# The last two batches of attention set between the steps of the leading expert's first product, and quarter-array products for all queries

## The chip, the core and the metric

The kernel runs on one core of one Trainium2 chip. The metric is the device time of that core in microseconds (us), from repeated executions. The engines are TensorE (PE, with its weight loads PEld), VectorE (DVE), ScalarE (ACT), GpSimd (POOL) and SyncE (SP), which here only issues transfers (DMA). Each engine works through its own instructions in order and waits on semaphores for the others.

## What is computed

Attention without a softmax, a normalisation per head, and then a mixture of eight experts of which each token takes one:

```python
def _attn_ref(q, k, v, g_norm):                 # q, k, v: 8 batches, 8 heads, 576 tokens, 64
    kv = np.einsum('bhsd,bhse->bhde', k, v)
    out = np.einsum('bhsd,bhde->bhse', q, kv)
    rms = np.sqrt(np.mean(out * out, axis=-1, keepdims=True) + 1e-06)
    return out / rms * g_norm

def _moe_ref(x, w_gate, w_output_gate, w1, w2): # x: 4608 tokens x 512; w1: 8 x 512 x 1024; w2: 8 x 1024 x 512
    logits = x @ w_gate
    e_idx = np.argmax(logits, axis=1)
    # gate_w: softmax probability of the chosen expert; eom: a sigmoid of x @ w_output_gate
    for e in range(E):
        mask = e_idx == e
        h = np.maximum(x[mask] @ w1[e], 0.0)
        out[mask] = gate_w[mask, None] * eom[mask, e, None] * (h @ w2[e])
```

## The kernel before

**Attention.** `p1_main` goes through the batches 0 to 7. `kv_part(b)` multiplies k and v of a batch (tile `kvps`, L474), ACT and DVE copy the result out (`aug`, `kvc`), `kvT_part` transposes it (`kvTps`), and `m_part` multiplies it with the two gates (`mps`, L501). The 4608 tokens are 36 tiles of 128 rows. `out_tile(g)` multiplies the queries of a tile with the `aug` of its batch (tile `ops`, L541), and ACT takes three pieces out of PSUM: the row itself (`xrow`, L546), its squares (`sq`, L548) and the gate products (`gp`, L549). DVE sums the squares (`ss`, L562). `ops`, `mps` and the experts' `hps` share two PSUM buffers of one pool, `ps_b`.

**Loads and stores.** All loads stand on SP's queue: k and v (`kvm`, four pieces of 512 KB to a batch, and `rem` for what remains), queries (`qT`, two tiles to a piece), and the weights (`wraw`). Rows `xrow` and their tails `xtail` are written to a table `xs` in HBM, from which an expert later gathers its rows (`xg`, an indirect DMA issued by POOL, L239). SP waits in order: a store that waits for its data holds all that is behind it.

**Routing.** The tiles form four groups of 10, 10, 4 and 12. `route(gi)` is a chain of small DVE operations for a group, with products on PE between (`rps`: counts; `tblps`: the table of rows, L749) and the operands `la` made by POOL, ACT and DVE (L719). It is a generator; `advance()` takes all open chains one stretch further, and the code calls it after each tile and at steps written out by hand. After the third group, that is after 24 tiles, the most loaded expert so far is known: the leading expert. Its first 384 rows are gathered (`gather(0)`), scaled by POOL (`xg`, L247), transposed (`tps`, L271) and split in a high and a low part (`xT`).

**Experts.** `RUNS` lists the stretches of rows: run 0 is the first 384 rows of the leading expert, run 1 its remaining 320, run 2 and on the other experts. `mm1(i, f)` is one of eight steps of the first product (`hps`, L308, twelve matmuls to a step); ACT and DVE make the high and low part of its result (`hT`, L317 and L318). `mm2(i, k)` is the second product for one tile of rows (`yps`, L350). Weights come as `wraw` and are split in `whi` (ACT, or DVE for the first) and `wlo` (DVE or POOL, L217 and L224); for the second product of the leading expert POOL makes all four `wlo`.

**What sets the order.** Inside `manual_schedule` the instructions of the named engines stay in the order in which the code issues them. Up to tile 36 the steps of the leading expert hang on the number of finished tiles (`HOOKS`: R is `advance`, G the gather, W the loads of w2, X the stores of the last rows, N the scaling, L one step of the leading expert, S one split of w2), and then the string `TAIL` sets them. `mm2(0, ...)` is issued after that, in the loop over `RUNS`, with the staging (`stage`) of run 1 between its matmuls; on PE its first ten matmuls come to stand ahead of the last three steps of the first product.

Of the kernel before, what the change touches and what calls it, by code (L numbers as in the profile page):

```python
# [11 lines left out]
F32 = mybir.dt.float32  # L12
# [9 lines left out]
P = 128  # L22
# [44 lines left out]

HOOKS = {15: 'R', 27: 'RR', 28: 'R', 31: 'RGW', 32: 'X', 34: 'NL'}
TAIL = "QLLLLRRRSLSRRSLLRRRLSLRRSRLSLL"
# [58 lines left out]
MAN = {ET.PE, ET.Activation, ET.DVE, ET.Pool}  # L131
# [3 lines left out]
def body(ctx: ExitStack, tc: tile.TileContext, kvm, rem, qT, wg, gn, w1, w2, kc, xs, tab, out):  # L135
# [191 lines left out]
    def mm2(i, k, events):  # L327
# [5 lines left out]
        ps = ps_y.tile([P, DM], F32, name="yps", tag=f"y{ny % 2}")  # L333
        ny += 1
# [18 lines left out]
        y = hp.tile([P, DM], F32, name="y", bufs=3)  # L353
# [11 lines left out]
        tc.add_to_no_dep_group("out", i_.ins)  # L365

# [80 lines left out]

    def load(spare):

        while loads and len(free) > spare:  # L450
            where, k, src = loads.pop(0)
            n = src.shape[0]
            if k in where:
                nc.sync.dma_start(out=where[k][P - n:], in_=src)
                continue
            t = take([P] + list(src.shape[1:]), F32, "ld")
            nc.sync.dma_start(out=t[:n], in_=src)
            where[k] = t
# [56 lines left out]
    def out_tile(g):  # L515
# [19 lines left out]
        for p in range(NP):  # L535
            for b, r0, m in parts:
                q0 = g % 2 * P + r0

                for u in range(2):
                    r = slice(u * D, (u + 1) * D)  # L540
                    nc.tensor.matmul(ps[r0:r0 + m, u, p * W:(p + 1) * W], qt[g // 2][r, p, q0:q0 + m],  # L541
                                     augs[b % 3][r, p, :], start=True, stop=True)
# [254 lines left out]
    def run_out(limit):  # L797
        nonlocal done_tiles
        if done_tiles < limit:
# [4 lines left out]
            advance()  # L804
# [3 lines left out]
            if lead_placed and opened[0] and (0, 1, 0) not in raw and (1, 0) not in wgt:  # L808
                for c in range(1):
                    wload(0, 1, c)  # L810
            for step in HOOKS.get(done_tiles, ""):
                act(step)

    def act(step):
        if step == "R":
            advance()
        elif step == "W":
            for c in range(4):
                wload(0, 2, c)
        elif step == "X":  # L820
            open_rows(1)
# [3 lines left out]
        elif step == "G":  # L825
            gather(0)
            behind.append(nc.gpsimd.memset(mark, 0.0))
            for c in range(1, 4):
                after_rows(wload(0, 1, c))
        elif step == "N":  # L830
            scale_rows(0)
        elif step == "S":
            next(lead2, None)
        else:
            next(lead, None)
# [337 lines left out]
```

## Time and profile before

| | us |
|---|---|
| median of three runs | 619.95 (618.67 to 620.07) |
| the profiled execution | 620.81 |
| its span, first to last instruction | 618.8 |
| PE busy | 566.5 (92%) |
| DVE, ACT, POOL busy | 263.2, 222.0, 164.0 |
| HBM read and written | 72.63 MB and 19.99 MB |

All durations come from the profiled execution, whose time lies 2.0 us above its span and 0.86 us above the median. A row of the timeline gives start, duration, engine, line, operation, tiles and sizes; in brackets stands the idle time of the engine before it and what ended it. The fp32 matmuls of the attention appear as two passes, so the counts there are double those of the program. PEclk is the clock that TensorE was granted, 1.00 being full speed.

### The profile page before, as it was taken

What the parts mean: (1) busy time and instruction counts of PE and PEld (TensorE: products, weight loads), DVE (VectorE), ACT (ScalarE), POOL (GpSimd) and SP (SyncE); (2) the same over time, 40 slices, a digit from 0 to 9 for tenths busy, and PEclk for the clock granted to TensorE, in tenths of its full rate; (3) what the DMA queues carried; (4) which work ended last, traced back from release to release, by engine and by line L of the source; (5) the groups of instructions that cost most, each with busy time, mean ns of one, the idle gap of its engine ahead of it and who ended that gap; (6) DMA issues with size and microseconds to landing.
All of it is one profiled execution on the core that took longest, in us unless ns stands there. A gap on an engine that the chain in (4) does not pass through costs nothing.

```text
span 618.8 us, 10459 instructions
## 1 busy us (share of the span) xinstructions
PE 566.5 (92%) x4179; PEld 506.3 (82%) x4179; DVE 263.2 (43%) x536; ACT 222.0 (36%) x413; POOL 164.0 (27%) x163
## 2 busy tenths in 40 slices
PE   3799978848999999999899999999999999999991
PEld 3688868747898998889789988998799889889881
DVE  2123688699425456225331453235135325424300
ACT  1335545634225334323331343234234423523310
POOL 2001044443832510630036117104500630110010
PEclk9958777579999999999999999999999999999996
DMA  8999991770564622349776332524432451110010
GB/s 271 367 409 407 405 366 49 246 285 7 166 231 138 202 89 90 87 169 35 16 159 199 115 122 91 172 69 138 145 112 74 135 181 68 53 52 2 0 47 14
DMA packets 39122, 92.53 MB, mean 150 GB/s; under 512 B 14418, under 2 KB 14546, under 8 KB 39072
## 3 DMA queue, kind: packets, MB, share of 16 engines
q1 hardware_dynamic: 32176, 71.63, 37.4%
q0 software_dynamic: 6464, 20.00, 10.2%
q8 instruction: 34, 0.56, 0.4%
q10 hardware_dynamic: 432, 0.21, 0.1%
q14 instruction: 16, 0.13, 0.1%
HBM read 72.63 MB, written 19.99 MB: 150 GB/s over the span
## 4 chain that ended last, share of the span: by engine, by line
PE 57%; issue 19%; DMA 10%; DVE 4%; POOL 3%; ACT 3%; another core or an unknown queue 2%; SPq 0%; POOLq 0%; DVEq 0%
PE hps L308 24%; PE yps L350 23%; PE ops L541 3%; PE kvps L474 3%; DMA ld<-kvm 3%; DMA xs<-xrow 2%; PE tps L271 2%; POOL out L361 2%; DMA ld<-qT 2%; DMA ld<-rem 2%; PE yps L345 1%; POOL xg L239 1%; DMA wraw<-w 1%; DMA xg<-xs,gidx 1%
## 5 line engine op out<-in xcount | busy, mean ns | idle before, releaser
L308 PE MATMUL hps<-xT,whi 128*128 128x320 f32 (+4 forms) x1024 | 197.3, 310 | 9.5 <-DVE hT L318 8.4
L350 PE MATMUL yps<-whi,hT 128*128 128x512 f32 (+2 forms) x592 | 195.9, 399 | 1.0 <-ACT whi L221 1.0
L308 PEld LDWEIGHTS hps<-xT,whi 128*128 128x128 f32 x1024 | 163.6, 191 | 11.9 <-DVE hT L318 9.1
L350 PEld LDWEIGHTS yps<-whi,hT 128*128 128x128 f32 (+2 forms) x592 | 111.3, 188 | 25.2 <-ACT whi L221 1.2
L308 PE MATMUL hps<-xT,wlo 128*128 128x320 f32 (+4 forms) x512 | 121.6, 309 | 0.0
L318 DVE SCALAR_TENSOR_TENSOR hT<-hps,hT 128x512 fp32r<-128x512 f32 (+5 forms) x112 | 59.2, 529 | 142.6 <-ACT hT L317 142.3
L350 PE MATMUL yps<-wlo,hT 128*128 128x512 f32 (+2 forms) x296 | 116.6, 394 | 0.8 <-DVE wlo L224 0.8
L317 ACT ACTIVATE hT<-hps 128x512 fp32r<-128x512 f32 (+5 forms) x112 | 52.5, 469 | 164.0 <-PE hps L308 121.6
L308 PEld LDWEIGHTS hps<-xT,wlo 128*128 128x128 f32 x512 | 89.0, 191 | 0.0
L361 POOL DMA_INDIRECT out<-y,oidx x42 | 44.8, 1068 | 154.2 <-ACT y L360 107.2
L239 POOL DMA_INDIRECT xg<-xs,gidx x42 | 43.2, 1029 | 137.5 <-PE tps L271 54.6
L350 PEld LDWEIGHTS yps<-wlo,hT 128*128 128x128 f32 (+2 forms) x296 | 55.7, 188 | 12.1 <-DVE wlo L224 1.1
L217 DVE SCALAR_TENSOR_TENSOR wlo<-wraw,gcol,whi 128x1024 fp32r<-128x1024 f32 x32 | 43.9, 1372 | 39.6 <-ACT whi L214 39.6
L247 POOL TENSOR_TENSOR xg<-xg 128x512 f32<-128x512 f32 (+3 forms) x40 | 44.0, 1102 | 43.9 <-DMA xg<-xs,gidx 43.5
L541 PE MATMUL ops<-aug,ld 64*128 64x80 f32 (+1 forms) x640 | 49.0, 327 | 5.8 <-ACT gp L549 5.7
L541 PEld LDWEIGHTS ops<-aug,ld 64*128 64x128 f32 (+1 forms) x640 | 44.5, 230 | 8.8 <-ACT gp L549 6.4
L360 ACT ACTIVATE y<-yps,tl 128x512 f32<-128x512 f32 (+2 forms) x37 | 25.5, 689 | 71.4 <-PE yps L350 68.4
L276 ACT CAST xT<-tps 128x512 fp32r<-128x512 f32 (+3 forms) x45 | 23.6, 530 | 67.6 <-PE tps L271 63.9
L277 DVE TENSOR_TENSOR xT<-tps,xT 128x512 fp32r<-128x512 f32 (+3 forms) x45 | 27.7, 617 | 46.9 <-ACT xT L276 43.3
L474 PE MATMUL kvps<-ld 128*64 128x64 f32 (+1 forms) x640 | 36.4, 300 | 11.1 <-DMA ld<-kvm 10.7
L474 PEld LDWEIGHTS kvps<-ld 128*64 128x64 f32 (+1 forms) x640 | 33.1, 209 | 14.0 <-DMA ld<-kvm 12.0
L224 DVE TENSOR_TENSOR wlo<-wraw,whi 128x1024 fp32r<-128x1024 f32 x28 | 34.3, 1226 | 13.5 <-ACT whi L221 6.7
(158 smaller groups left out, 403.2 us busy)
## 6 DMA issues: line engine op xcount, KB each, us to landing
wraw<-w SPq DMA_DIRECT2D x64, 512.0 KB, 3.2
ld<-kvm SPq DMA_DIRECT2D x32, 512.0 KB, 10.2
ld<-qT SPq DMA_DIRECT2D x18, 512.0 KB, 10.2
xs<-xrow SPq DMA_DIRECT2D x13, 512.0 KB, 10.4
xs<-xrow SPq DMA_DIRECT2D x2, 1280.0 KB, 15.2
ld<-rem SPq DMA_DIRECT2D x3, 512.0 KB, 10.2
xg<-xs,gidx POOLq DMA_INDIRECT x42
out<-y,oidx POOLq DMA_INDIRECT x42
```

What stands on the lines that cost most here:

```text
L217: eng.scalar_tensor_tensor(out=lo, in0=r, scalar=gcol[:, 0:1], in1=hi.bitcast(F32), op0=ALU.mult, op1=ALU.subtract)
L224: eng.tensor_tensor(out=lo, in0=r, in1=hi.bitcast(F32), op=ALU.subtract)
L239: nc.gpsimd.indirect_dma_start(out=x[:M, :], out_offset=None, in_=rows, in_offset=bass.IndirectOffsetOnAxis(ap=gidx[:M, p, t:t + 1], axis=0))
L247: eng.tensor_tensor(out=v, in0=v, in1=f, op=ALU.mult)
L277: nc.vector.tensor_tensor(out=lo[:, :, c0:c0 + M], in0=v, in1=hi.bitcast(F32)[:, :, c0:c0 + M], op=ALU.subtract)
L308: nc.tensor.matmul(ps[:, j, :n], w[:, o:o + P], x[d][:, j * N:j * N + n], start=(d == 0 and k == 0), stop=(d == 3 and k == 2))
L317: nc.scalar.activation(hh, x, AF.Relu)
L318: nc.vector.scalar_tensor_tensor(out=v(h[:, l:l + n]), in0=x, scalar=0.0, in1=hh.bitcast(F32), op0=ALU.max, op1=ALU.subtract)
L350: nc.tensor.matmul(ps[:M], a, b, start=(f == 0 and k == 0), stop=(f == 7 and k == 2))
L361: i_ = nc.gpsimd.indirect_dma_start(out=out, out_offset=bass.IndirectOffsetOnAxis(ap=oidx[:M, p, t:t + 1], axis=0), in_=y[:M], in_offset=N ...
L474: nc.tensor.matmul(ps[u * D:(u + 1) * D, p * D:(p + 1) * D], k, v, start=(s == 0 and p == 0), stop=(s == 4 and p == NP - 1))
L541: nc.tensor.matmul(ps[r0:r0 + m, u, p * W:(p + 1) * W], qt[g // 2][r, p, q0:q0 + m], augs[b % 3][r, p, :], start=True, stop=True)
```

## The change

The first 24 tiles and the batches 0 to 5 go as before, with no step of the leading expert among them. The loads of the last two batches and of the queries from tile 24 on go into a second list, `later`. Then a string, `SCRIPT`, sets everything until the end of the leading expert's first 384 rows: routing of the first three groups to its end (`QF`), five of the late loads, weights and the gather, batch 6 (`K`, `T`, `M`), and the eight steps of the first product with twelve tiles (`o`) and batch 7 among them. The splits of w2 and the routing of the last group come after the last tile, with the three `mm2(0, ...)` between the routing's stretches (`Y`). Run 1 is gathered, scaled and staged after that, by itself. SP joins the engines whose order is the code's. The products of `out_tile` are cut into quarters of the array: 64 query rows by 64 contraction rows each, instead of 128 by 64, which before was so only where a batch ended inside a tile. The second products of run 0 take their PSUM from `ps_b`.

```diff
-HOOKS = {15: 'R', 27: 'RR', 28: 'R', 31: 'RGW', 32: 'X', 34: 'NL'}
-TAIL = "QLLLLRRRSLSRRSLLRRRLSLRRSRLSLL"
+FIRST = LEAD_TILES
+SCRIPT = ("QF" "ddddd1G1" "K" "NL" "T" "LLL" "dd1" "L" "L" "MX" "o" "dd1" "L" "o" "dd" "L" "o" "o" "dd" "L" "o" "K"
+          "L" "T" "o" "dd" "L" "M" "o" "22" "o" "L" "o" "o" "22" "L" "o" "o" "S" "Q" "SRSRS" "YRRRR" "YRRRR" "YRRRRRR")
...
-MAN = {ET.PE, ET.Activation, ET.DVE, ET.Pool}
+MAN = {ET.PE, ET.Activation, ET.DVE, ET.Pool, ET.SP}
...
-        ps = ps_y.tile([P, DM], F32, name="yps", tag=f"y{ny % 2}")
-        ny += 1
+        if i == 0:
+            ps = ps_b.tile([P, 2, 512], F32, name="yps0", tag="big")[:, 0]
+        else:
+            ps = ps_y.tile([P, DM], F32, name="yps", tag=f"y{ny % 2}")
+            ny += 1
...
+    cut = lambda w, k: (k if w is qt else 2 * k if w is rt else k[0])
+    later = [l for l in loads if cut(l[0], l[1]) >= (FIRST // 2 if l[0] is qt else FIRST * P // S + 1)]
+    loads = [l for l in loads if not any(l is x for x in later)]
...
-                q0 = g % 2 * P + r0
-                for u in range(2):
-                    r = slice(u * D, (u + 1) * D)
-                    nc.tensor.matmul(ps[r0:r0 + m, u, p * W:(p + 1) * W], qt[g // 2][r, p, q0:q0 + m],
-                                     augs[b % 3][r, p, :], start=True, stop=True)
+                for c0 in range(r0, r0 + m, D):
+                    q0 = g % 2 * P + c0
+                    for u in range(2):
+                        r = slice(u * D, (u + 1) * D)
+                        nc.tensor.matmul(ps[c0:c0 + D, u, p * W:(p + 1) * W], qt[g // 2][r, p, q0:q0 + D],
+                                         augs[b % 3][r, p, :], start=True, stop=True)
...
-            advance()
+            if done_tiles <= FIRST:
+                advance()
...
+        elif step == "F":
+            while routing:
+                advance()
...
+        elif step in "12":
+            c = (w1s if step == "1" else w2s).pop(0)
+            d = wload(0, int(step), c)
+            if behind:
+                after_rows(d)
+        elif step == "d":
+            fetch(later)
+        elif step == "K":
+            state["kvc"] = kv_part(b)
...
+        elif step == "o":
+            run_out(NT)
...
+        elif step == "Y":
+            mm2(0, state.setdefault("y", 0), {})
...
-        for b in range(B):
-            lim = tiles_ready(b - 1) if b else 0
+        for b in range(B - 2):
+            lim = min(tiles_ready(b - 1) if b else 0, FIRST)
...
-        while done_tiles < NT:
-            run_out(NT)
-        for step in TAIL:
+        while done_tiles < FIRST:
+            run_out(FIRST)
+        for step in SCRIPT:
             act(step)
...
                 gather(1)
                 scale_rows(1)
-                for _ in lead:
-                    next(lead2, None)
-                for _ in lead2:
-                    pass
+                for h in hT[0]:
+                    give(h)
+                for x in range(len(tiles_of(1))):
+                    stage(1, x)
+                continue
```

Three places in the order of the instructions carry the prediction. The first is SP's queue around the third group's tails (`xtail` of 4 tiles, written when that group is routed). Before:

```order
L771 DMA xs<-xrow 128x2x512 x2
L771 DMA xs<-xtail 128x10x16
L771 DMA xs<-xtail 128x4x16
L185 TENSOR_LOAD epos
L185 ISA x2
L194 ISA
L194 DMA wraw<-w 128x1024
```

and after the change:

```order
L788 DMA xs<-xrow 128x2x512
L788 DMA xs<-xtail 128x10x16
L788 DMA xs<-xtail 128x4x16
L473 DMA ld<-rem 128x1024
L473 DMA ld<-kvm 128x1024 x4
L188 TENSOR_LOAD epos
L188 ISA x2
L197 ISA
L197 DMA wraw<-w 128x1024
```

The loads of batch 6 now stand behind the store that waits for the routing of group three, and ahead of the first weights of the leading expert.

The second is PE from the leading expert's transposes (`tps`) into its first product (`hps`). Before, the attention (`ops`) was done by then:

```order
L541 MATMUL ops<-aug_115,ld 64x80 x2
L541 MATMUL ops<-aug_116,ld 64x80 x2
L541 MATMUL ops<-aug_116,ld 128x80 x32
L271 MATMUL tps<-ident,xg 128x128 x12
L308 MATMUL hps<-xT,whi 128x384 x2
L308 MATMUL hps<-xT,wlo 128x384
```

After, of the eight steps of `hps` the first two are shown, the repeated rows left out:

```order
L490 MATMUL kvps<-ld 64x64 x40
L505 MATMUL kvTps<-ident,kvc 128x128 x2
L274 MATMUL tps<-ident,xg 128x128 x12
L311 MATMUL hps<-xT,whi 128x384 x2
L311 MATMUL hps<-xT,wlo 128x384
...
L517 MATMUL mps<-gw,kvT 64x16 x8
L558 MATMUL ops<-aug_117,ld 64x80 x16
L311 MATMUL hps<-xT,whi 128x384 x2
L311 MATMUL hps<-xT,wlo 128x384
...
L558 MATMUL ops<-aug_117,ld 64x80 x16
```

Batch 6's product now stands ahead of the transposes, and the tiles from 24 on stand between the steps.

The third is PE from the last `tblps` of the last group's routing to run 1's first product (`hps` of 320 columns). Before:

```order
L749 LDWEIGHTS la
L749 MATMUL tblps<-rrc,la 128x96
L308 MATMUL hps<-xT,whi 128x384 x2
...
L271 MATMUL tps<-ident,xg 128x128 x4
L350 MATMUL yps<-whi,hT 128x512
...
L271 MATMUL tps<-ident,xg 128x64 x4
L350 MATMUL yps<-whi,hT 128x512
...
L308 MATMUL hps<-xT,whi 128x320 x2
```

After:

```order
L356 MATMUL yps_2135<-whi,hT 128x512
L693 LDWEIGHTS row_106
...
L766 LDWEIGHTS la
L766 MATMUL tblps<-rrc,la 128x96
L356 MATMUL yps_2246<-whi,hT 128x512
...
L274 MATMUL tps<-ident,xg 128x128 x8
L274 MATMUL tps<-ident,xg 128x64 x4
L311 MATMUL hps<-xT,whi 128x320 x2
```

The table of the last group stood ahead of three steps of the first product and nearly all second products; now two of the three second products (`yps`) stand ahead of the counts (`row`, for `rps`), one behind the table, and the transposes of run 1 follow with nothing between them and its first product.

More of the change, by code (lines that the diff above doesn't have):

```diff
@@ L352, in mm2 @@
                 e()
-        y = hp.tile([P, DM], F32, name="y", bufs=3)
+        y = take([P, DM], F32, "y0") if i == 0 else hp.tile([P, DM], F32, name="y", bufs=3)
         if M == T:
@@ L365, in mm2 @@
         tc.add_to_no_dep_group("out", i_.ins)
+        if i == 0:
+            give(y)
     def lead_run():
@@ L446, in body, with fetch @@
                 nq += 1
+    cut = lambda w, k: (k if w is qt else 2 * k if w is rt else k[0])
+    later = [l for l in loads if cut(l[0], l[1]) >= (FIRST // 2 if l[0] is qt else FIRST * P // S + 1)]
+    loads = [l for l in loads if not any(l is x for x in later)]
+    later.sort(key=lambda l: (12.5 + (l[1] - FIRST // 2) // 2 if l[0] is qt else 2 * l[1] + 0.1 if l[0] is rt else 2 * l[1][0]))
     def load(spare):
         while loads and len(free) > spare:
[L451 to L458, printed above, removed]
+            fetch(loads)
+    def fetch(loads):
+        where, k, src = loads.pop(0)
+        n = src.shape[0]
+        if k in where:
+            nc.sync.dma_start(out=where[k][P - n:], in_=src)
+            return
+        t = take([P] + list(src.shape[1:]), F32, "ld")
+        nc.sync.dma_start(out=t[:n], in_=src)
+        where[k] = t
     def kv_part(b):
@@ L807, in run_out @@
                 open_rows(0)
[L808 to L812, printed above, removed]
+    w1s, w2s = list(range(4)), list(range(4))
+    state = {"b": B - 2}
     def act(step):
+        b = state["b"]
         if step == "R":
             advance()
[L817 to L821, printed above, removed]
+        elif step == "F":
+            while routing:
+                advance()
         elif step == "Q":
@@ L849, in p1_main @@
                 run_out(lim)
-        while done_tiles < NT:
-            run_out(NT)
-        for step in TAIL:
+        while done_tiles < FIRST:
+            run_out(FIRST)
+        for step in SCRIPT:
             act(step)
+        assert not later and done_tiles == NT and not w1s and not w2s and state["y"] == len(tiles_of(0))
         while routing:
             advance()
+        for _ in lead:
+            assert False
+        for _ in lead2:
+            assert False
     vec = nc.vector
@@ L1061, in body @@
                 mm2(i, k, at.get(k, {}))
-            if i == 0:
-                for h in hT[0]:
-                    give(h)
-            if i > 0:
-                for c in range(4):
-                    drop(2, c)
+            for c in range(4):
+                drop(2, c)
     main.close()
```

14 lines of the change are left out of this document (10 added, 4 removed).

## The prediction

> **What bounds the kernel now.** I read PE in stretches first, then each engine's timeline from 30 to 180 us, and last the order of the changed program. The stretches (PE and PEld, DVE, ACT, POOL busy, then the clock, the DMA share and GB/s):
>
> ```profile
> 90.00:110.00 20.00, 17.06 (x270) 15.83 (x273) 17.63 (x81) 9.50 (x28) 7.47 (x12) 0.67 0.32 81
> ...
> 110.00:117.60 7.60, 7.60 (x76) 7.10 (x68) 6.08 (x12) 4.98 (x12) 6.04 (x6) 0.50 0.75 229
> 117.60:137.00 19.40, 9.60 (x38) 8.34 (x36) 15.83 (x24) 9.06 (x16) 8.46 (x5) 0.68 0.91 332
> 137.00:158.00 21.00, 18.46 (x107) 16.86 (x108) 18.80 (x57) 7.49 (x17) 8.08 (x8) 0.91 0.11 22
> ...
> 175.00:606.00 431.00, 428.35 (x2479) 383.07 (x2478) 164.31 (x270) 149.69 (x236) 107.17 (x101) 1.00 0.38 105
> ...
> 174.69 0.45 PE L308 MATMUL hps<-xT,whi 128*128 128x320 f32 x2
> ```
>
> From 175 us on PE is never without work for longer than 2.65 us in all, at full clock. What follows run 1's first product, which begins at 174.69, is the same work in both programs. So the change is worth what it moves that one start; a gain later is at most 2.65 us. Before it, the only large gap is 117.6 to 137, half idle.
>
> I follow the start through four stretches: A, until the leading expert's gather; C, from there to its first product; D, that product with twelve tiles in it; E, from the last tile to run 1.
>
> **A: until the gather.** Before, it is issued at 110.86. Rows of PE, ACT, DVE, POOL and SP:
>
> ```profile
> 35.62 1.30 PE L541 MATMUL ops<-aug,ld 64*64 64x80 f32 x30
> 37.46 3.71 PE L541 MATMUL ops<-aug,ld 64*128 64x80 f32 x32
> 44.96 4.18 SPq L457 DMA_DIRECT2D ld<-kvm  x4
> ld<-kvm SPq DMA_DIRECT2D x32, 512.0 KB, 10.2
> 76.22 0.61 ACT L548 ACTIVATE sq<-ops 128x512 f32<-128x512 f32 x1
> 84.33 0.59 ACT L546 COPY xrow<-ops 128x512 f32<-128x512 f32 x1 [0.22 <-PE ops L541]
> 85.44 0.40 ACT L491 COPY kvT<-kvTps 128x256 f32<-128x256 f32 x1
> 84.14 0.42 DVE L482 COPY kvc<-kvps 128x256 f32<-128x256 f32 x1 [1.88 <-ACT aug L480]
> 84.48 0.67 DVE L562 TENSOR_REDUCE ss<-sq 128x8 f32<-128x512 f32 x1
> 85.08 1.48 DVE L618 TENSOR_TENSOR gp<-gp,xtail 128x1280 f32<-128x1280 f32 x1
> 94.44 6.29 POOL L719 TENSOR_SCALAR la<-ni,rlon 128x128 bf16<-128x128 f32 x10 [10.87 <-DVE rlon L698]
> 107.96 0.17 DVE L742 TENSOR_TENSOR xtail<-rdn 128x4 f32<-128x4 f32 x1
> 110.86 1.08 POOL L239 DMA_INDIRECT xg<-xs,gidx  x1 [5.09 <-DVE oidx L900]
> ```
>
> Quarters: 30 of a tile's 32 passes took 1.30, so 1.39 a tile, where two tiles of the half form took 3.71. That is 0.9 us less for each such pair, and three stand between 37 and 69 us: 2.7. Where PE is quicker, ACT sets the pace: its three pieces of one tile go from 84.33 to 85.44, 1.1 us. The other tiles give some 1.3 us together. So tile 19's squares, done at 76.83, come 4 us sooner. (Batch 5's last piece is issued at 49.1 and lands 10.2 later, at 59.3; its product ran at 68.93. The loads would allow 9.6 us and no more.)
>
> Next, DVE: from 76.83 to the second group's product `gp` at 85.08 it waited 1.88 us for batch 6 and copied its `kvc`, 0.34. Batch 6 is gone from here: 2.2 us less.
>
> Then the chain from 85.08 to the gather, 25.8 us. PE has nothing beside it now, since batch 6 stands behind the last table. Out of it fall five sums of tiles from 24 on (0.6 each, as from 84.48 to 85.08); but POOL's ten `la` (6.29) and the tail's store (107.96 to 110.86) stay. I take 2.9 off; the bounds are 0 and, with DVE's idle time taken out as well (20 less 17.63 from 90 to 110), 5.4. Sum of A: 4 + 2.2 + 2.9 = 9.1, the gather at 101.8 (97 to 105).
>
> **C: gather to first product.** Before, 110.86 to 122.74, 11.9 us:
>
> ```profile
> 109.60 10.37 SPq L194 DMA_DIRECT2D wraw<-w  x8
> 115.02 1.94 DVE L217 SCALAR_TENSOR_TENSOR wlo<-wraw,gcol,whi 128x1024 fp32r<-128x1024 f32 x1
> 119.50 0.41 DVE L277 TENSOR_TENSOR xT<-tps,xT 128x256 fp32r<-128x256 f32 x1
> ...
> 123.58 0.42 DVE L277 TENSOR_TENSOR xT<-tps,xT 128x256 fp32r<-128x256 f32 x1 [0.44 <-ACT xT L276]
> 122.74 1.15 PE L308 MATMUL hps<-xT,whi 128*128 128x384 f32 x2 [0.46 <-ACT xT L276]
> ```
>
> The five loads of batch 6 are issued behind the third group's tail, 2.9 us before the gather, and the first weights behind them. At 1.3 us each (10.37 for eight) and some 2 us of landing the sixth arrives 10 us later, at 109. PE holds the transposes behind batch 6's product, and DVE holds `xT` behind `kvc` and the split of those weights (some 0.9 for its high part and 1.9, to 112); the three tiles' `xT` took from 119.50 to 124.0, and the product began at 122.74, 3.2 us after the first and ahead of the last. With a little for the product's own wait that makes 116, or 14.2 us after the gather; bounds 11.9 (all of it hidden) and 17.
>
> **D: first product with twelve tiles.** A step's first and last rows, a mixed tile, a batch's product, and the two that empty a step's PSUM:
>
> ```profile
> 150.77 0.61 PE L308 MATMUL hps<-xT,whi 128*128 128x384 f32 x2 [0.67 <-DVE hT L318]
> ...
> 152.81 0.34 PE L308 MATMUL hps<-xT,wlo 128*128 128x384 f32 x1
> 60.04 0.72 PE L541 MATMUL ops<-aug,ld 64*64 64x80 f32 x30
> 56.41 3.73 PE L474 MATMUL kvps<-ld 128*64 128x64 f32 x77
> L317 ACT ACTIVATE hT<-hps 128x384 fp32r<-128x384 f32 x8 | 3.9, 488 | 18.4 <-PE hps L308 18.4
> L318 DVE SCALAR_TENSOR_TENSOR hT<-hps,hT 128x384 fp32r<-128x384 f32 x8 | 4.3, 550 | 0.0
> ```
>
> Eight steps of 2.2, twelve tiles of 0.8, batch 7's product 3.9, its transposes and two gate products 1.3: 32.4 us at full clock. The first step runs at half (1.15 for the pair that took 0.61), 1.9 more: 34.3. Steps, tiles and gate products share two buffers, so each waits until the one two places ahead is emptied: a tile needs 1.2 us of ACT, a step 0.49 and 0.55. Walking the printed order with these durations, PE waits 3.2 us in all: 37.5. Bounds: 34.3, and 42 if batch 7 also waits for its loads, which SP holds behind the store of tiles 24 and 25 (one landing of 10.2 less the 5.5 us of PE work between). The last tile leaves PE at 116 + 37.5 = 153.5.
>
> The Trainium skill, "TensorEngine Tiling (Array Packing)", Theoretical Speedup, allows up to twice for a small output side; by that a tile would take 0.54 instead of 0.8, and D 3 us less. The row of 0.72 for 30 passes says otherwise, and its PSUM Bottleneck section, that emptying then sets the pace, is what ACT's 1.1 us shows.
>
> **E: last tile to run 1.** POOL and DVE in contention, then the routing's later rows, a second product, and run 1's gather and start:
>
> ```profile
> 129.66 4.66 POOL L224 TENSOR_TENSOR wlo<-wraw,whi 128x1024 fp32r<-128x1024 f32 x2 [1.50 <-ACT whi L221]
> 125.83 2.39 DVE L589 TENSOR_SCALAR ra<-ss 128x96 f32<-128x96 f32 x1
> 132.16 2.28 DVE L609 TENSOR_TENSOR ru<-ru,ra 128x96 f32<-128x96 f32 x1
> 142.09 0.26 DVE L648 TENSOR_TENSOR ohb<-rsc,rsx 128x96 bf16<-128x96 f32 x1
> 161.93 5.48 PE yps L350 x24
> 145.05 0.25 DVE L689 TENSOR_TENSOR rw<-rps,ohb 128x96 f32<-128x96 f32 x1
> 149.42 0.69 PE L749 MATMUL tblps<-rrc,la 128*128 128x96 bf16 x12
> 153.74 0.16 DVE L919 CAST gidx<-gif 128x3 int32<-128x3 f32 x1
> 154.18 1.39 POOL L239 DMA_INDIRECT xg<-xs,gidx  x1 [1.16 <-DVE t L933]
> 158.75 0.66 PE L271 MATMUL tps<-ident,xg 128*128 128x128 f32 x4 [0.38 <-DVE xg L247]
> ```
>
> Before, all this lay beside the first and second products. Now, counted from the last tile:
> - The four splits of w2 stand behind ACT's pieces of it. POOL's `wlo` start at 2.4 and take 2.4 each, to 12; the first second product needs each for a quarter of its matmuls and ends at 13.4. The second adds 5.5: 18.9. The counts `rps` stand behind it on PE, to 19.6.
> - DVE's chain to them is no quicker. From `ra` at 125.83 to `ohb` at 142.35 were 16.5 us, of which three operations took 2.3 to 2.4 instead of 0.26 while POOL split (6.3), and 1.7 went to the leading expert: 8.5 alone. With 1.9 for the last tile's squares and sum, and four such operations held (8 us), `ohb` comes at 18.
> - From `rw` at 145.05 to the table's end at 150.11 are 5.1 us: 24.7. The third second product now begins, and ends at 30.2.
> - From the table's end to the gather 4.1 us, of which one DVE operation lost 1.8 to POOL, which is now idle there, though the tail must still land: 3.3, the gather at 28.
> - From a gather to a first product on three tiles: 11.9 was measured, with the first weights' split in it; here the first tile needs 4.6 us to its transposes (154.18 to 158.75), and each of the other two some 3 more. I take 11: 39.
> - PE stands idle twice for 5 us and more, so second product and first step begin at half clock, as at 122.74: 2 more. E is 41, between 36.5 and 44.
>
> **Costed at nothing.** The quarters double the attention's matmuls from 16 passes a tile to 32; the 0.72 for 30 holds their issue already. The second products' PSUM comes from the two shared buffers: both are free once ACT has emptied the last two tiles, 1.2 us after them, under the wait for `wlo`. SP's fixed order holds two more things: w2's loads stand behind the store of tiles 26 to 30, some 8 us of PE work ahead of the splits, and run 1's gather waits for the store of the last five tiles, issued 26 us before it. If w2 were late, E would start later by as much, at most a landing of 10.2 less 8, 2 us.
>
> **The sum.** 101.8 + 14.2 + 37.5 + 41 = 194.5, against 174.69: 19.8 us later. 620.81 + 19.8 = 640.6 for an execution like the profiled one, and with the median 0.86 below it, 640.
>
> **Rivals.**
> - *Faster: the routing ends with the 24th tile.* The forecast needs the chain of 25 us behind tile 23 to stay. Were it worked off beside the tiles, as the first group's is before, the gather could follow at 80, and the end would come at 618. It decides at a gather before 82. For it: POOL's ten `la` had waited 10.87 us for DVE's turn. Against: the second group's chain cannot start before tile 19, and DVE was busy 17.63 of the 20 us from 90 to 110.
> - *Half the price.* The loads pace A (5.6 us more), and D waits for no buffer (3.2): 631. For it: nothing but ACT's pace stands against the loads.
> - *D at half clock.* From 110 to 117.6 PE was busy all the time and still had 0.50, with small products alone. If the mixture does the same, eight steps cost 1.9 more each and batch 7 somewhat: 15 us, 655. Against: dense steps began at 122.74 and 137.04, and 137 to 158 has 0.91. The Trainium skill, "TensorE: Matmul & The Clock Gate", Part 1, has the clock rise after some 3.4 us of sustained work and fall after an idle window; by it D runs at full clock behind its first step, as summed. The row of 110 to 117.6 does not agree with it.
> - *No change.* The four differences cancel; only by chance, 620.
>
> **Chances.** Forecast 0.72 (its own range 632 to 648), half price 0.10, half clock 0.09, no change 0.03, faster 0.06. A measurement of this kernel can tell 0.3% from no change, 1.9 us. Faster 0.06, same 0.03, slower 0.91. The range, 626 to 653, goes to the half-price case with some of A's and E's bounds and nearly to the half clock.
>
> **What would show it.** In the changed profile: the gather near 102, with PE all but idle from 77 to 104; the first step near 116; the last tile near 153, with PEclk 1.0 from 120; POOL's four `wlo` in a row, DVE operations of 2.4 beside them; PE gaps behind the last tile, behind the counts and ahead of run 1, 17 us together; run 1 near 194, and the rest as long as before. It is wrong if the gather comes before 90, or if run 1's gather is issued beside the second products.

## The result and the profile after

The changed kernel takes 650.58 us (median of four runs, 649.22 to 653.78) against 620.01 for the kernel before beside it: a ratio of 1.050, 95% interval 1.045 to 1.055. That is 30.6 us slower; 19.8 were forecast. The time lies in the range of 626 to 653, and above the forecast's own range of 632 to 648. The profiled execution took 649.22 with a span of 647.4 and is the quickest of the four. Of the 30.6 us, 28.6 are between the two spans, 2.2 between the medians and the profiled executions (1.4 above the one after, 0.8 below the one before), less 0.2 outside the spans. The same program on another chip (number 8 below) takes 649.42, the median of three runs; a fourth, at 659.17, was in the chip's slower state and is left out.

Busy time by stretches, first of the changed kernel, cut at the gather, the first product, the last tile and run 1, then of the kernel before, cut at its own (PE, PEld, DVE, ACT, POOL busy, then the clock, the DMA share and GB/s):

```profile
0.00:57.00 57.00, 35.16 (x920) 30.08 (x920) 14.45 (x35) 19.18 (x49) 5.55 (x8) 0.94 0.99 362
57.00:105.21 48.21, 20.08 (x492) 16.02 (x492) 34.60 (x127) 17.85 (x50) 15.43 (x22) 0.68 0.43 144
105.21:122.85 17.64, 9.03 (x95) 7.37 (x95) 4.18 (x11) 2.51 (x7) 6.23 (x7) 0.50 1.02 399
122.85:161.48 38.63, 32.91 (x594) 28.55 (x594) 15.74 (x25) 21.56 (x49) 0.00 (x0) 0.96 0.53 185
161.48:201.48 40.00, 25.34 (x113) 19.04 (x112) 29.40 (x70) 11.86 (x24) 23.84 (x20) 0.78 0.46 152
201.48:647.40 445.92, 430.03 (x2480) 385.12 (x2480) 165.74 (x271) 149.50 (x235) 112.59 (x107) 0.98 0.38 100
```

```profile
0.00:57.00 57.00, 41.47 (x628) 36.67 (x629) 14.37 (x35) 19.58 (x51) 4.24 (x8) 0.81 0.98 360
57.00:110.86 53.86, 45.29 (x800) 41.60 (x798) 39.52 (x136) 27.76 (x78) 15.29 (x23) 0.75 0.76 275
110.86:122.74 11.88, 9.80 (x74) 8.70 (x73) 8.23 (x16) 7.46 (x20) 7.29 (x7) 0.50 0.86 276
122.74:174.69 51.95, 41.31 (x208) 35.94 (x209) 36.74 (x81) 17.06 (x31) 28.95 (x24) 0.89 0.49 159
174.69:618.80 444.11, 428.66 (x2481) 383.38 (x2479) 164.31 (x270) 150.19 (x236) 108.24 (x102) 0.98 0.37 103
```

Run 1 starts at 201.48 instead of 174.69, 26.8 us later. Up to there PE has 15.4 us less to do (122.5 busy instead of 137.9; the attention's products alone fell from 49.1 to 31.1, where the quarters by themselves, number 1 below, bring them to 36.6), and stands idle 42.1 us more (79.0 instead of 36.8). Of the 42.1, 6.3 lie before 57 us, 19.6 in the drain of the routing, 6.5 between gather and first product, and 9.7 behind that. What follows run 1's start is 1.8 us longer.

| stretch | forecast | measured |
|---|---|---|
| A, to the gather | 101.8 | 105.2 |
| C, gather to first product | 14.2 | 17.6 |
| D, first product to the last tile | 37.5 | 38.6 |
| E, last tile to run 1 | 41 | 40.0 |
| run 1's first product | 194.5 | 201.5 |

Two rows of the kernel before say what the start was there. Its last tile leaves PE at 117.67, ahead of the first product, and its last second product is followed by run 1's first product (174.69) without a wait; from run 1's gather at 154.18 to there PE is busy for 20.1 of 20.5 us.

```profile
109.02 8.65 PE L541 MATMUL ops<-aug,ld 64*64 64x80 f32 x96
174.46 0.39 PE L350 MATMUL yps<-whi,hT 128*128 128x512 f32 x1
```

Rows of the changed kernel's timeline, in groups by stretch. A, the idle time that was not forecast, and the gather:

```profile
50.38 25.74 SPq L788 DMA_DIRECT2D xs<-xrow  x10
60.68 0.59 ACT L563 COPY xrow<-ops 128x512 f32<-128x512 f32 x1 [9.92 <-DMA xs<-xrow]
62.23 0.42 DVE L498 COPY kvc<-kvps 128x256 f32<-128x256 f32 x1 [11.03 <-ACT aug L496]
62.71 0.69 PE L505 MATMUL kvTps<-ident,kvc 128*128 128x128 f32 x2 [6.13 <-DVE kvc L498]
105.21 1.08 POOL L242 DMA_INDIRECT xg<-xs,gidx  x1 [4.58 <-issue]
```

ACT waits 9.92 us to copy a tile's row out, because the memory slot given to that row still holds another row whose store has not landed. (The kernel keeps a list of free slots and hands out the one that was given back first. A row's slot goes back to the list where the code issues its store. The code holds the stores back until no load is left to issue: here until after the 5th tile, before until after the 19th. So the row of the 13th tile is given the slot of the very first row, whose store is still under way.) Behind ACT wait DVE's copy and PE's transposes, 6.13 us in which PE has nothing. C:

```profile
103.42 2.11 SPq L473 DMA_DIRECT2D ld<-kvm  x4
108.62 1.12 PE L490 MATMUL kvps<-ld 128*64 128x64 f32 x16 [6.14 <-DMA ld<-kvm]
114.66 2.17 PE L490 MATMUL kvps<-ld 128*64 128x64 f32 x32 [1.52 <-DMA ld<-kvm]
112.08 1.04 POOL L250 TENSOR_TENSOR xg<-xg 128x512 f32<-128x512 f32 x1 [3.15 <-DMA xg<-xs,gidx]
114.84 1.04 POOL L250 TENSOR_TENSOR xg<-xg 128x512 f32<-128x512 f32 x1 [0.25 <-DMA xg<-xs,gidx]
122.85 1.15 PE L311 MATMUL hps<-xT,whi 128*128 128x384 f32 x2 [0.46 <-ACT xT L279]
```

Batch 6's last load lands at 114.66, 9.1 us after the end of its issue at 105.53, and the first gathered rows 6.9 us after theirs (105.21 to 112.08), where the kernel before began scaling at 114.53, 3.7 us behind its gather. The DMA engines are full in this stretch (1.02). D and E:

```profile
137.19 0.62 PE L311 MATMUL hps<-xT,whi 128*128 128x384 f32 x2 [0.79 <-ACT gp L566]
160.70 0.78 PE L558 MATMUL ops<-aug,ld 64*64 64x80 f32 x32 [0.46 <-DVE hT L321]
163.81 9.39 POOL L227 TENSOR_TENSOR wlo<-wraw,whi 128x1024 fp32r<-128x1024 f32 x4 [47.93 <-ACT whi L224]
163.88 2.40 DVE L616 SCALAR_TENSOR_TENSOR ru<-ry 128x96 f32<-128x96 f32 x1
171.00 2.32 DVE L622 SCALAR_TENSOR_TENSOR ry<-ru,ry 128x96 f32<-128x96 f32 x1
180.09 0.26 DVE L665 TENSOR_TENSOR ohb<-rsc,rsx 128x96 bf16<-128x96 f32 x1
185.42 1.12 PE L766 MATMUL tblps<-rrc,la 128*128 128x96 bf16 x12 [4.46 <-DVE rrc L753]
189.75 1.08 POOL L242 DMA_INDIRECT xg<-xs,gidx  x1 [4.81 <-DVE oidx L938]
197.17 0.77 PE L274 MATMUL tps<-ident,xg 128*128 128x128 f32 x4 [2.50 <-POOL xg L250]
201.48 1.09 PE L311 MATMUL hps<-xT,whi 128*128 128x320 f32 x2 [0.46 <-ACT xT L279]
```

In D PE waits in pieces of 0.3 to 0.8 us, 5.7 in all; the clock is 0.96 over D and 1.00 from 126 us on, behind the first step. In E the last routing runs by itself. PE waits for w2's parts first (2.31, 1.64 and 0.71), then for the routing at the table (4.46), and after that for run 1's rows (2.50 and 2.42).

### The profile page after: what moved, and what is told of

Its sections match the earlier page's. It is cut to its first block, busy times and chain, and to the rows that moved or that the text cites. A ratio compares the mean times of both kernels' runs of the same rounds, so it can differ in the third digit from the quotient of the medians.

```text
span 647.4 us, 11500 instructions
## 1 busy us (share of the span) xinstructions
PE 552.5 (85%) x4691; PEld 486.2 (75%) x4691; DVE 264.1 (41%) x536; ACT 222.5 (34%) x413; POOL 163.6 (25%) x163
## 3 DMA queue, kind: packets, MB, share of 16 engines
q1 hardware_dynamic: 32176, 71.63, 36.6%
## 4 chain that ended last, share of the span: by engine, by line
PE 51%; issue 19%; DMA 11%; POOL 6%; DVE 5%; ACT 3%; another core or an unknown queue 2%; SPq 1%; POOLq 0%; ACTq 0%; DVEq 0%
PE hps L311 25%; PE yps L356 20%; DMA ld<-kvm 5%; POOL la L736 2%; PE tps L274 2%; POOL out L367 2%; PE ops L558 2%; DMA xs<-xrow 2%; DMA ld<-qT 1%; DMA wgs<-wg 1%; POOL xg L242 1%; PE yps L351 1%; PE kvps L490 1%; DMA xg<-xs,gidx 1%
## 5 line engine op out<-in xcount | busy, mean ns | idle before, releaser
L242 POOL DMA_INDIRECT xg<-xs,gidx x42 | 42.4, 1010 | 139.4 <-PE tps L274 51.1
L250 POOL TENSOR_TENSOR xg<-xg 128x512 f32<-128x512 f32 (+3 forms) x40 | 42.7, 1070 | 45.5 <-DMA xg<-xs,gidx 45.2
L490 PE MATMUL kvps<-ld 128*64 128x64 f32 (+1 forms) x640 | 32.4, 268 | 22.3 <-DMA ld<-kvm 20.5
L490 PEld LDWEIGHTS kvps<-ld 128*64 128x64 f32 (+1 forms) x640 | 28.2, 177 | 26.2 <-DMA ld<-kvm 22.8
L280 DVE TENSOR_TENSOR xT<-tps,xT 128x512 fp32r<-128x512 f32 (+3 forms) x45 | 27.7, 617 | 44.9 <-ACT xT L279 44.7
L558 PE MATMUL ops<-aug,ld 64*64 64x80 f32 x1152 | 31.1, 255 | 9.9 <-ACT gp L566 6.6
L558 PEld LDWEIGHTS ops<-aug,ld 64*64 64x64 f32 x1152 | 26.2, 150 | 14.1 <-ACT gp L566 5.3
## 6 DMA issues: line engine op xcount, KB each, us to landing
ld<-qT SPq DMA_DIRECT2D x18, 512.0 KB, 10.5
```

The lines of the kernel that those rows point to most:

```text
L242: nc.gpsimd.indirect_dma_start(out=x[:M, :], out_offset=None, in_=rows, in_offset=bass.IndirectOffsetOnAxis(ap=gidx[:M, p, t:t + 1], axis=0))
L250: eng.tensor_tensor(out=v, in0=v, in1=f, op=ALU.mult)
L280: nc.vector.tensor_tensor(out=lo[:, :, c0:c0 + M], in0=v, in1=hi.bitcast(F32)[:, :, c0:c0 + M], op=ALU.subtract)
L490: nc.tensor.matmul(ps[u * D:(u + 1) * D, p * D:(p + 1) * D], k, v, start=(s == 0 and p == 0), stop=(s == 4 and p == NP - 1))
L558: nc.tensor.matmul(ps[c0:c0 + D, u, p * W:(p + 1) * W], qt[g // 2][r, p, q0:q0 + D], augs[b % 3][r, p, :], start=True, stop=True)
```

## The experiments

My theory after this reading: A, C and E each have a cause of their own, and what is taken off one of them arrives at the end. The rival: the start is one chain with several members, and a gain at one place is waited away at the next. The table has the times at which the stretches end, from one profile each, and the medians; kernels 1 to 4, 5 to 8, 9 and 10, and 11 and 12 ran on one chip each, with the kernel before at 618.96, 618.80, 619.78 and 619.22.

| kernel | gather | first product | last tile ends | run 1's gather | run 1 | span | median |
|---|---|---|---|---|---|---|---|
| before | 110.86 | 122.74 | 117.67 | 154.18 | 174.69 | 618.8 | 620.01 |
| after | 105.21 | 122.85 | 161.48 | 189.75 | 201.48 | 647.4 | 650.58 |
| 1 before, quarters | 106.83 | 118.82 | 113.88 | 150.28 | 170.82 | 616.7 | 618.28 |
| 2 after, halves | 108.63 | 126.15 | 167.94 | 196.19 | 210.36 | 656.0 | 657.14 |
| 3 stores opened later | 101.41 | 118.77 | 157.48 | 185.78 | 199.72 | 644.5 | 649.49 |
| 4 loads ahead | 104.69 | 115.16 | 155.96 | 184.26 | 197.63 | 644.9 | 644.12 |
| 5 w2 split early | 105.47 | 122.98 | 161.78 | 184.03 | 195.85 | 642.9 | 645.97 |
| 6 w2's low part on DVE | 106.04 | 123.58 | 161.84 | 188.65 | 201.47 | 648.6 | 650.11 |
| 7 = 3 + 4 + 5 | 101.85 | 112.71 | 151.92 | 174.16 | 186.18 | 634.1 | 637.34 |
| 8 after again | 105.06 | 122.54 | 160.75 | 189.07 | 200.38 | 645.5 | 649.42 |
| 9 a batch in the drain | 107.70 | 126.03 | 155.93 | 179.40 | 193.38 | 641.4 | 644.11 |
| 10 the same, one step | 113.48 | 123.77 | 154.03 | 177.54 | 191.29 | 641.2 | 641.16 |
| 11 = 9, loads earlier | 108.06 | 118.92 | 149.45 | 172.94 | 185.96 | 634.1 | 636.92 |
| 12 before, splits last | 108.24 | 120.21 | 115.28 | 148.13 | 174.48 | 619.1 | 620.58 |

**1 and 2: the quarters alone.** The loop of `out_tile` is put into the kernel before, and taken out of the changed one:

```diff
-                    nc.tensor.matmul(ps[r0:r0 + m, u, p * W:(p + 1) * W], qt[g // 2][r, p, q0:q0 + m],
+                for c0 in range(r0, r0 + m, D):
...
+                        nc.tensor.matmul(ps[c0:c0 + D, u, p * W:(p + 1) * W], qt[g // 2][r, p, q0:q0 + D],
```

> The kernel before, with only its attention products cut into quarters (the products of one tile keep the PE for about 0.9 us instead of 1.4; 18 us of PE time over the 36 tiles). Theory 1 (the loads pace the first 70 us, then the drain of the routing and the gather pace the front; PE's time there is covered): run 1's first product starts within 2 us of 174.7, time 618 to 621. Rival (PE is what the tiles wait for): most of 9 us between 57 and 111 comes off, 610 to 615.

> The changed kernel with half-array products as before (one matmul of 64 or 128 queries in place of two of 64). Theory 1: the first 24 tiles are paced by loads and stores, so the gather moves by at most 2 us; the 12 tiles in the first product add 12 x 0.5 = 6 us to a PE that is 85% busy there: 655 to 658. Rival: the first product is paced by the ACT copies, 33 of which stand there, and 650 stays (649 to 652).

In the kernel before, the quarters bring gather, first product and run 1 forward by 3.9 to 4.0 us each, but the span is only 2.1 shorter and the time the same: ratio 0.998 (0.995 to 1.001). So neither expectation held for the start, and the first for the time. In the changed kernel the halves cost 8.9 us at run 1: 3.4 in A, 3.2 in D (a tile takes 1.12 there instead of 0.78), 2.4 in E, where run 1's second tile of rows comes 4.87 us late to PE instead of 2.50. The time is 657.14, ratio 1.060 (1.052 to 1.068; the changed kernel's interval reaches 1.055). It lies in the range of the first theory, but by luck: D gave about half of the expected 6 us, A more than the 2 that it was allowed, and E was not in the theory. So the quarters are worth something in the changed kernel, and are not what made it slower.

**3: the slot of the row.**

```diff
-            if not loads and not opened[0]:
+            if not loads and not opened[0] and done_tiles >= 16:
```

> The changed kernel with the stores of the rows opened after 16 tiles instead of at the end of the loads (10 tiles). Theory 1: the idle 6.1 us of PE at 56 to 63 is tile 14's xrow waiting 9.9 us for the slot of a store that queues behind the loads; it goes, gather(0) comes at 99 to 100 instead of 105.2 and the time falls to 644 to 646. Rival: the stores then collide with the end of the drain, or the gather waits for loads anyway; less than 2 us comes off.

```profile
57.16 0.44 PE L505 MATMUL kvTps<-ident,kvc 128*128 128x128 f32 x2 [0.37 <-DVE kvc L498]
101.41 1.07 POOL L242 DMA_INDIRECT xg<-xs,gidx  x1 [4.58 <-issue]
195.44 1.11 PE L274 MATMUL tps<-ident,xg 128*128 128x128 f32 x4 [4.67 <-POOL xg L250]
```

The wait is gone, and the gather comes at 101.41, near the 101.8 of the prediction; the expectation had 99 to 100. How it went I had not thought of: SP's first store is still issued at 50 us, since the queue holds nothing else there. But with the stores opened after the 16th tile in the code instead of the 5th (not the 10th, as the expectation has it), the row gets a slot that a load has left and not that of a store on its way. 4.1 us arrive at the first product, 4.0 at the last tile and at run 1's gather, but 1.8 at run 1: its second tile of rows comes 4.67 us late to PE instead of 2.50. The time, 649.49, ratio 1.049 (1.042 to 1.056), cannot be told from that of the changed kernel; 644 to 646 was expected. By the time the rival is right, by the gather the theory.

**4: the loads of batch 6.**

```diff
-SCRIPT = ("QF" "ddddd1G1" "K" "NL" "T" "LLL" "dd1" "L" "L" "MX" "o" "dd1" "L" "o" "dd" "L" "o" "o" "dd" "L" "o" "K"
+SCRIPT = ("Q" "ddddd" "F" "1G1" "K" "NL" "T" "LLL" "dd1" "L" "L" "MX" "o" "dd1" "L" "o" "dd" "L" "o" "o" "dd" "L" "o" "K"
```

> The changed kernel with the five loads of the seventh batch issued ahead of the drain of the routing, not behind its last store. Theory 1: from the gather to the first product it took 17.6 us, since kvps waits for these loads and the gathered rows land 6.9 us after their issue behind 2.5 MB of loads; with the loads landed it is 11 to 13 us, the time 644 to 646. Rival: PE's order and the routing's own work set it (the half clock, the scaling on POOL): 16 us or more, 649 to 652.

They are issued from 82.89 on, while the DMA engines have little to do (a share of 0.16 from there to 101 us in the changed kernel). From the gather to the first product it now takes 10.5 us instead of 17.6. The first product begins 7.7 us sooner; 5.5 of these are left at the last tile, since D runs at half clock until 124.9 (0.88 over D instead of 0.96), and 3.9 at run 1. The time is 644.12, ratio 1.037 (1.030 to 1.045), within the expected 644 to 646.

**5 and 6: POOL's low parts beside the last routing.** Number 5 issues w2's loads ahead of the last queries' and splits between the last tiles; number 6 leaves the place and changes the engine:

```diff
-          "L" "T" "o" "dd" "L" "M" "o" "22" "o" "L" "o" "o" "22" "L" "o" "o" "S" "Q" "SRSRS" "YRRRR" "YRRRR" "YRRRRRR")
+          "L" "T" "o" "22" "dd" "L" "22" "M" "o" "o" "L" "S" "o" "S" "o" "L" "S" "o" "S" "o" "Q" "RR" "YRRRR" "YRRRR" "YRRRRRR")
```

```diff
-SPLITS = ['VV', 'AV', 'AV', 'AV', 'AP', 'AP', 'AP', 'AP']
+SPLITS = ['VV', 'AV', 'AV', 'AV', 'AV', 'AV', 'AV', 'AV']
```

> The changed kernel with w2's four chunks loaded ahead of the last loads of the queries and split (ACT high part, POOL low part) between the last six tiles of the first product, where POOL had nothing to do, not behind the last tile. Theory 1: behind the last tile (161.5 to 201.5) the DVE chain of the last routing is the bound, and four of its small operations take 2.31 to 2.40 us there instead of 0.26 because POOL's low parts run beside them; without them the gather of run 1 comes 8 us sooner, at 181 to 182, the time falls by 6 to 9 us, to 642 to 645. Rival: the low parts now stand beside the hT and sum operations of DVE in the first product, which gets longer by as much (38.6 to 44 us or more), and the time stays within 2 us.

> The changed kernel with w2's low parts on DVE in place of POOL, at the same place. Theory 1: the four small operations of 2.31 to 2.40 us go back to 0.26 (8.3 us less) and four low parts of about 1.3 us come onto DVE (5.2 more): the gather of run 1 comes 3 us sooner, the time falls by 2 to 3 us. Rival: it is not POOL's neighbourhood that makes these four long, and the time grows by 5 us.

Rows of number 5: POOL's low parts, the operation that took 2.40, run 1's gather and its first product.

```profile
156.40 4.71 POOL L227 TENSOR_TENSOR wlo<-wraw,whi 128x1024 fp32r<-128x1024 f32 x2 [39.49 <-ACT whi L224]
166.50 0.26 DVE L616 SCALAR_TENSOR_TENSOR ru<-ry 128x96 f32<-128x96 f32 x1
184.03 1.08 POOL L242 DMA_INDIRECT xg<-xs,gidx  x1 [4.78 <-DVE oidx L938]
195.85 1.09 PE L311 MATMUL hps<-xT,whi 128*128 128x320 f32 x2 [0.46 <-issue]
```

All four operations are back at 0.26, in number 6 too (its first at 167.48), where only the engine of the low parts was changed: it is POOL's work that makes them long. The Trainium skill, "SBUF — State Buffer", section "SBUF: two separate sides", has DVE and GpSimd share a pair of ports that one instruction holds to its end. The rows agree: 2.31 to 2.40 us each beside low parts of 2.36 to 2.40.

What this is worth depends on where the low parts go. In number 5, E falls from 40.0 to 34.1, D stays at 38.8, and 5.6 us arrive at run 1 (4.5 against number 8, the changed kernel on the same chip). That is less than expected: run 1's gather comes at 184.03 and not at 181 to 182, and the time, 645.97, is just above 642 to 645. Against the 649.42 of number 8 it cannot be told apart: the ratios to before are 1.043 (1.036 to 1.050) and 1.052 (1.042 to 1.061). In number 6 four low parts of 1.22 come onto DVE itself, the gather comes 26.8 behind the last tile instead of 28.3, and run 1 not sooner: 650.11, ratio 1.049 (1.041 to 1.056), no change that can be told, where 2 to 3 us were expected.

**7 and 8: all three, and the changed kernel beside them.**

> The changed kernel with the three edits together: stores of the rows opened after 16 tiles, the seventh batch loaded ahead of the drain, and w2 split between the last tiles. Theory 1 (the three stretches add up): run 1's first product at 201.5 - 4 - 6 - 8 = 183 to 186, the time 631 to 635, still above the kernel before (619), because PE idles 20 us in the drain which attention covers there. Rival (each gain is lost again further on, as 2 of the 4 us of the stores were): 638 to 642.

> The changed kernel unaltered, beside the three, so that they are compared on one chip: 648 to 653.

```profile
112.71 1.15 PE L311 MATMUL hps<-xT,whi 128*128 128x384 f32 x2 [0.46 <-ACT xT L279]
174.16 1.08 POOL L242 DMA_INDIRECT xg<-xs,gidx  x1 [4.78 <-DVE oidx L938]
186.18 1.10 PE L311 MATMUL hps<-xT,whi 128*128 128x320 f32 x2 [0.46 <-issue]
151.90:186.18 34.28, 22.76 (x116) 17.90 (x112) 22.03 (x70) 9.65 (x23) 19.65 (x18) 0.83 0.51 164
186.18:634.10 447.92, 431.36 (x2480) 385.69 (x2480) 165.90 (x271) 149.64 (x235) 112.93 (x107) 0.98 0.37 100
```

Run 1 starts 14.2 us sooner than in number 8 and the time is 12.1 lower: 637.34 against 649.42; ratio to before 1.031 (1.023 to 1.038) against 1.052 (1.042 to 1.061). One by one the three edits moved run 1's start by 1.8, 3.9 and 5.6, 11.2 in all; together they move it by 15.3 on the same reckoning, so none takes from another. They are about 12 of the 30 us. The expected 631 to 635 was missed, mostly in the stretch behind run 1's start, 447.9 us here and 444.1 in the kernel before. Number 1 has 445.9 there with the same later program as the kernel before, so some of this is not the change's; why it varies is open.

**9, 10 and 11: does attention fill the drain?** The rest of the loss looked like PE's idle time in the drain, from which the attention had been taken away. So I put one batch and six tiles back there, and left the last batch in D. Number 9 has two routing steps behind each of those tiles; its edits against number 7:

```diff
-FIRST = LEAD_TILES
+FIRST = 30
...
-        for b in range(B - 2):
+        for b in range(B - 1):
...
+            if LEAD_TILES < done_tiles <= FIRST:
+                advance()
...
+SCRIPT = ("Q" "ddddddd" "F" "1G1" "NL" "LLL" "1" "L" "L" "X" "1" "L" "L" "K" "L" "T" "o" "22" "L" "M" "22" "o" "L" "o" "S" "L" "o" "S" "L" "o" "S" "L" "o" "S" "Q" "RR" "YRRRR" "YRRRR" "YRRRRRR")
```

Number 10 is without the second `advance()`, one step behind each tile. Number 11 is number 9 with the seven loads (`d`) out of the string and behind the 25th tile:

```diff
+            if done_tiles == 25:
+                while later:
+                    fetch(later)
```

> The kernel of the three edits, with the attention of the seventh batch (its K and V products and six tiles) put back among the steps of the routing's drain, two steps behind each tile; the last batch alone (six tiles) stays in the first product. Theory 1 (the change moved PE work from a stretch where PE stands idle behind DVE and POOL, 78 to 102, into one in which PE is the bound): the first product loses six tiles and one batch's products, 38.4 to 26 to 30 us, the gather comes at most 4 us later than 101.9, and the time falls by 5 to 9 us to 628 to 632. Rival (ACT's copies and DVE's sums of six tiles lengthen the drain by what the product gives back): gather at 108 to 112, time 635 to 640.

> The same with one step of the routing behind each of the six tiles, so that PE reaches the last group's products behind the tiles. Theory 1: PE is idle there anyway, the gather moves by less than 3 us against the version with two steps, and the time by less than 3 us. Rival: the routing's order decides, gather 5 us or more later, time up by as much.

> The version with one batch in the drain and two steps behind each tile, with the last batch's seven loads issued behind the 25th tile, when the DMA engines stand idle, and not between the drain's last stores and the gather. Theory 1 (there the loads queued ahead of the gathered rows, so the way from the gather to the first product took 18.3 us where the three edits had 10.9): it takes 10 to 12 us again, the gather stays at 107 to 108, run 1's first product comes at 184 to 187, the time is 633 to 638, no better than the three edits alone (637), since the drain lengthens by about 6 of the 8.5 us that the first product gets shorter. Rival (the loads then hold up the stores of the rows or the tails as the gather's): gather at 110 or later, 640 to 645.

```profile
113.48 1.08 POOL L241 DMA_INDIRECT xg<-xs,gidx  x1 [8.81 <-issue]
108.06 1.07 POOL L241 DMA_INDIRECT xg<-xs,gidx  x1 [5.12 <-DVE oidx L942]
57.00:108.06 51.06, 31.45 (x782) 26.48 (x782) 38.13 (x134) 24.25 (x67) 13.93 (x23) 0.70 0.80 286
118.92:149.40 30.48, 28.48 (x386) 25.78 (x386) 11.94 (x19) 16.14 (x33) 4.73 (x2) 0.90 0.37 132
```

(The first row is of number 10, the others of number 11.) Number 9 starts run 1 7.2 us later than number 7, for two reasons: the gather came 5.9 us later, and the seven loads fell on it, so that 18.3 us passed to the first product. Its time is 644.11 (1.039, 1.034 to 1.044; the interval overlaps that of number 7), and not the expected 628 to 632. In number 10 (641.16; 1.033, 1.027 to 1.039) the loads stood ahead of the last tail's store, and the gather, which needs that store, came at 113.48; neither expectation had this reason, and the time did not rise with the gather as the rival had it. Number 11, with the loads out of the way, gives the clean answer: D is 8.7 us shorter, the gather 6.2 later, E 2.2 longer, run 1 0.2 sooner, and the time is 636.92 (1.028, 1.022 to 1.034) against 637.34 of number 7, all as expected. PE's idle time in the drain is 19.6 us of 51.1 (number 7: 21.3 of 44.9): seven to eight microseconds of PE work went in, and the drain grew by six. My theory of free room in the drain falls. That the tiles' sums on DVE and copies on ACT hold up the routing's chain is the reason that the rows leave, though no run separates them.

**12: a version of the kernel before.** The same contention stands in the kernel before (DVE operations of 2.28 to 2.46, and hT behind them). So: quarters, w2's low parts on DVE, and the splits behind the routing.

```diff
-TAIL = "QLLLLRRRSLSRRSLLRRRLSLRRSRLSLL"
+TAIL = "QLLLLRRRLRRLLRRRLLRRRLSSLSLS"
...
-SPLITS = ['VV', 'AV', 'AV', 'AV', 'AP', 'AP', 'AP', 'AP']
+SPLITS = ['VV', 'AV', 'AV', 'AV', 'AV', 'AV', 'AV', 'AV']
```

> The kernel before with quarters, and with w2's four splits moved behind the last steps of the routing and their low parts on DVE in place of POOL. Theory 1 (POOL's low parts stretch three routing operations of DVE from about 0.25 to 2.28 to 2.46 us, and hT behind them holds PE for 7.0 us): the three go back to 0.25, the wait of PE at 126 to 133 shrinks to under 2 us, run 1's first product comes at 164 to 167 against 170.8, the time is 611 to 615. Rival (the splits are then late for the second product, or the later runs give it back, as most of the 3.9 us of the quarters were): 616 to 620.

```profile
125.25 0.26 DVE L609 TENSOR_TENSOR ru<-ru,ra 128x96 f32<-128x96 f32 x1
128.12 0.61 PE L308 MATMUL hps<-xT,whi 128*128 128x384 f32 x2 [1.98 <-DVE hT L318]
133.45 0.66 PE L681 MATMUL rps<-ohb,ones 128*128 128x96 bf16 x12 [2.85 <-DVE ohb L648]
156.70 1.11 PE L271 MATMUL tps<-ident,xg 128*128 128x128 f32 x4 [6.21 <-DVE tl L267]
```

The operations are short again and the wait of 7.0 in number 1 is one of 1.98. But PE then waits 2.85 for the routing and 6.21 for run 1's rows, ahead of which it used to have work; run 1 starts at 174.48, later than in number 1. The rows are late by their slots: by the code the first tile's rows take the slot of w2's third piece, which is now split at 148.48, so that their gather is issued only at 152.40, behind three others. The time is 620.58, ratio 1.003 (1.000 to 1.006). The gain became a new wait, and the rival's 616 to 620 is about right, though of its two reasons neither is this one. None of the versions beats the kernel before.

## Why the prediction was right, and where it was short

The direction was right, and so was its reason: run 1's first product decides, and it comes later because the last routing no longer has the first product beside it. The size was 10.8 us short. Of these, 7.0 are in the start, 1.8 behind it, and the remaining 2.0 in how single executions lie to their medians. Two terms of the sum were too small, A and C, by 3.4 us each.

- **A** (101.8; 105.2). The term that failed is the 4 us "sooner" for tile 19's squares. These squares end at 76.24, only 0.6 sooner. The quarters do give the 4 us (the squares end at 72.64 in number 3); but the sentence beside it, that the loads allow 9.6 us, looked at loads alone. The rows of finished tiles need slots too, and the changed code opens the stores at an earlier tile. That cost PE 6.1 us; without it (number 3) the gather is at 101.4. The other two terms hold: from the second group's `gp` to the gather it took 22.7 us (82.50 to 105.21) where I had 22.9.
- **C** (14.2; 17.6, above the upper bound of 17). The place was right, the price of a load was not: I let five loads land at 1.3 us each, and forgot that the gathered rows go over the same full DMA engines and that weights and queries follow. The last piece took 9.1 us from its issue. Number 4 takes the loads away and has 10.5, below the lower bound of 11.9: that bound held a weight split and tiles of the kernel before.
- **D** (37.5; 38.6). The sum is right within 1.1 us, partly by luck: PE is idle for 5.7 us where 3.2 were forecast, and busy for 32.9 where the sum had 34.3 (batch 7's product takes 3.3 at full clock, not 3.9). Behind its first step it ran at a clock of 1.00, so the rival of half clock did not happen, though its 655 us lie nearer to the measured time than the forecast's 640. By the rule of the Trainium skill that the prediction named ("TensorE: Matmul & The Clock Gate", Part 1) this was to be expected, and here the trace agrees. A tile's 32 passes take 0.78, the 0.8 of the sum.
- **E** (41; 40.0). Nearly every member came as written: the last `wlo` ended at 11.7 behind the last tile (12), `ohb` began at 18.6 (18), the table ended at 25.1 (24.7), the gather was issued at 28.3 (28). Four operations of DVE were held, as the sum had it, at 8 us; in number 5, where they are not, E is 5.9 shorter.
- **"The rest as long as before"**: 1.8 longer. Run 1's first product runs at half clock until about 207, where before it began at full clock (1.09 for its first pair instead of 0.45). But number 1 begins it at full clock too, and its rest is as long, 445.9; so the cause of the 1.8 is open.
- **Costed at nothing**: w2 was not late (ACT goes from its last `gp` to `whi` at 162.67 without a gap), the PSUM cost nothing. The rivals: faster needed a gather before 82, half price needed no waits in D; neither is in the trace.
- **The last sign of being wrong** was badly put. Run 1's gather is issued at 189.75, beside the third second product (186.32 to 194.10), and the sum itself had it so (28, in a product from 24.7 to 30.2). What would have spoken against the forecast is a gather beside the first and second of them.

So the loss has two parts: about 12 us that are not the idea's (the slot, the loads' place, the splits' place; number 7 against number 8), shown by edits that take them away, and 18.5 us that are left (637.34 against 618.80). Of the 18.5, 11.5 are at run 1's start (186.18 against 174.69), 3.8 behind it, and the rest in how single executions lie to their medians.

The 11.5 are read from the two traces; no run puts the routing back beside the first product and keeps the rest. In number 7 the first product begins 10.0 us sooner than before, but run 1's gather 20.0 later. The last routing needs the last tile. Before, that tile left PE at 117.67, the gather followed 36.5 us later, and the first product ran beside it. In number 7 the routing is quicker, 22.2 us, but its tile ends with the first product, at 151.92. Behind the gather 8.5 us come back, because before PE still had second products to do there.

## What to carry to other kernels

Before work is moved between the steps of a later stage, look for the chain that starts when that work ends: here twelve tiles could well be fitted into a product at full clock, but the routing behind them, 22 us of small operations, lost its cover. Idle time of one engine need not be room: in number 11 eight microseconds of work put into it lengthened the stretch by six, it seems because the work also needs the engines on which that engine waits. And where a pool hands out memory in the order of the code, moving a store in the code changes which slot a later tile gets, and so what it waits for.

## What the runs showed of the hardware

- A small store or a gather can pay for the loads that are issued just ahead of it. With seven loads ahead of the last tail, the gather was issued 7.0 us after that tail (number 10); with the same loads behind the tail it was 2.8 (number 9). With five loads issued just before the gather its first rows came after 6.9 us (the changed kernel), without them after 3.8 at most (number 4).
- DVE's small operations of 128x96 took 2.31 to 2.40 us beside POOL's low parts and 0.26 without them, whether the low parts were moved away (number 5) or given to DVE (number 6).
